# Attention and a mixture of attention experts on one core: later dues for input loads and weights, earlier dues for transposing transfers

## The chip, the cores and the metric

The kernel runs on one core of one Trainium2 chip. The metric is the device time of one execution, in microseconds (us). A core has a matrix engine (TensorE, PE in the profile), a vector engine (VectorE, DVE), a scalar engine for functions such as tanh and exp (ScalarE, ACT), a general engine (GpSimd, POOL) and a small one that issues transfers (SyncE, SP). Each takes its instructions in the order of the program and waits for the others by semaphores. A DMA is a transfer that an engine issues and DMA engines carry out.

## The reference

```python
def _attn_ref(q, k, v, cap):                 # q, k, v: 8 x 12 x 448 x 64, cap = 30
    scores = np.matmul(q, k.transpose(0, 1, 3, 2)) / np.sqrt(64)
    scores = cap * np.tanh(scores / cap)
    attn = softmax(scores)                   # over the last axis
    return np.matmul(attn, v)

x = attn_out.transpose(0, 2, 1, 3).reshape(8, 448, 768)

def _moe_ref(x, w_gate, wq, wk, wv, wo):     # 4 experts, 2 chosen for each row
    logits = x @ w_gate                      # 768 -> 4
    w = softmax(the 2 largest logits)
    for e in range(4):
        q, k, v = x @ wq[e], x @ wk[e], x @ wv[e]        # 768 -> 64
        a = causal_softmax(q @ k.transpose(0, 2, 1) / 8)
        out += chosen(e) * w[e] * (a @ v @ wo[e])        # 64 -> 768
```

The first part is soft-capped attention for 8 batches of 12 heads. Its result x feeds the second part, four small attention experts, of which a gate picks two for each row. The output is 8 x 448 x 768 in 32-bit floats. All inputs are 32-bit; the kernel works in 16-bit floats inside.

## The kernel before

**Pieces.** Two heads make a pair p; there are 48, six to a batch. The pairs of the last batch are cut into two halves of rows, so that there are 54 pieces, numbered from 0; up to 41, piece and pair have one number. A piece goes through these steps:

1. Loads (`load_part`, L273; `add_load`, L314). Two pairs share a set of seven transfers on SP: k, q, two tails of k, v, two tails of v. Pairs 0 to 3 have a list of their own (L306); the others are made by the loop of L328 to L334, for p = 4, 6, 8 and so on, and go into four staging buffers in turn.
2. Casts to 16 bits on POOL (`add_cast`, L362): q (L350), k (L354), v (L360). For pairs 0 and 1 other engines do some.
3. Transposes of q and k (`add_tr`, L431). Up to pair 8 they are matmuls on PE (L398 for q), evicted by DVE. From pair 9 on, k is transposed by a transposing DMA on SP (`a_trd`, L423), and from pair 34 on q is too. "trK" below is the transpose of pair K.
4. Scores (`a_fill`, L502) by PE, into two PSUM tiles in turn, three banks and two banks; so a whole piece takes three tiles, called K.0, K.1 and K.2 in the text.
5. Tanh of each such tile (L513) and one exp for the piece (L522) by ACT.
6. The product with v (PV, L535 and L540) by PE, normalised by DVE (L549, L550), transposed into xT (L563, evicted at L576).

**The mixture.** When all six pieces of a batch are done, `add_batch` (L877) adds its experts: values and gate logits (vps, L620; memset of the value tile's column of ones on POOL, L629, then DVE's copy, L631), the gate on DVE, q and k of the experts (qps and kps, L724), copies of the mask on POOL (mb, L668) that a matmul and DVE turn into masked q, powers for the gate's softmax on POOL (L682 and on), score fills (L743), one exp for each half (L750), causal masking on POOL (L758), PV, o on DVE (L797), additions on POOL (L805), wops (the product with wo, L832), eviction to ob (L846), and a store on SP. The last batch is done half by half (`add_last`, L1160): its late projections are named tX, its last product lwo. The first half of the experts' work of batch b runs beside the attention of batch b + 1.

**Weights.** `add_weight` (L1297) issues them from POOL, as DMAs that turn 32 into 16 bits on the way (L1301): the gate and four wv (into wvg), then two wq and two wk, two wq and two wk, four wo. Their dues are 14, 20, 26 and 32.

**Who sets the order.** The class `Sched` (L25 to L180) is a planner that runs while the program is built. Every step is added as a unit (`add`, L51) with an engine, a duration, the units that it depends on, a `due` (its rank), `after` (a time before which the planner doesn't start it) and, for transfers, `land` (bytes, which the planner sends through a single modelled line of 2.15e5 bytes per us, L107 to L109). The planner keeps a clock for each engine. At each step it takes, among the ready units that could start first on an engine, the one with the smallest due (`pick`, L123). It emits instructions in that planned order. None of these times exists on the chip: only the order does, and the waits for what each instruction uses. Score fills and ACT's work stand outside the dues: fills go in the order of pieces, and other PE work is put between where the plan says that ACT has enough ahead.

Dues come from `nom` (L254 to L259), a nominal start for each piece, about 5.5 us apart in the first batch, and 5.8 after it. A pair's loads are due 40 before its start (L334), and the planner may issue them as soon as their buffer is free. Casts of q and k are due 14 or 20 before, v 4 before; transposes 8 before; transposing DMAs six ahead of that (L447).

```python
        if u["land"]:
            self.dma = max(self.dma, s + 2.0) + u["land"] / 2.15e5
            t = self.dma + 0.1
```

**Semaphores of transfers.** Transfers of SP and ACT use eight semaphores in rotation, and so do the weights on POOL: a transfer waits for the eighth before it.

Of the kernel before, what the change touches and what calls it, by code (L numbers as in the profile page):

```python
# [15 lines left out]
DEBUG = False  # L16
NAUX = 3
PV = (9.0, 5.0, 2.0)
TB = (0.0, 0.0)
PACE = (1.0, 1.0)  # L20
LATE = 3
T0D = -4.0


class Sched:  # L25
# [25 lines left out]
    def add(self, key, eng, dur, deps, due, fn, *args, take=None, give=None, slack=None, land=0,  # L51
            after=0.0, alt=False):
        deps = [d for d in deps if d is not None]
        u = dict(
            key=key, eng=eng, dur=dur, deps=deps, due=due, fn=fn, args=args, take=take, give=give,
            slack=self.SLACK if slack is None else slack, land=land, n=0, r=0.0, after=after, alt=alt,
        )
        self.count += 1
        for d in deps:
            if d not in self.done:  # L60
                u["n"] += 1
                self.wait.setdefault(d, []).append(u)
        if u["n"] == 0:
            self.arm(u)
# [119 lines left out]
def kernel(  # L184
# [13 lines left out]
    nc = tc.nc  # L198

    B, H, S, Dh = q.shape  # L200
# [35 lines left out]
    add = sch.add  # L236
# [24 lines left out]
    def nomp(p):  # L261
        return nom[of[p][0]]
# [38 lines left out]
    def nbytes(n, which):  # L301
        t = {"q": 224 * 0.055, "k": 256 * 0.045, "v": 256 * 0.045}.get(which, 64 * 0.03)
        return n * t / 16 * 2.15e5
# [7 lines left out]
        ("q", 0, 1, "ACT"), ("kt1", 0, 2, "ACT"), ("vt1", 0, 2, "ACT"),  # L311
    ]

    def add_load(p, n, w, due, e, deps):  # L314
        add(
            ("ld", w, p), e, 0.62, deps, due, load_part, p, n, w,
            nc.scalar if e == "ACT" else nc.sync, land=nbytes(n, w),
        )
        for i in range(n):
            ld_of[p + i, w] = ("ld", w, p)  # L320

    last = {}
    for x, (w, p, n, e) in enumerate(FIRST):
        d = [last.get(e)] + ([("zst", w[0], p // 2)] if len(w) > 1 else [])
        d += [("table",)] if e == "ACT" and x > 17 else []
        add_load(p, n, w, -100.0 + x, e, d)
        last[e] = ("ld", w, p, "issued")
    for p in range(4, NP, 2):  # L328
        deps = []
        if p // 2 >= NST:  # L330
            deps = [("cast", w, p - 2 * NST + i) for i in range(2) for w in CASTS]
        for w in PARTS:
            d = deps + [last["SP"]] + ([("zst", w[0], p // 2)] if len(w) > 1 and p < 2 * NST else [])
            add_load(p, 2, w, nomp(p) - 40.0, "SP", d)  # L334

    warm = const.tile([128, 512], f16, name="warm")
    ident = const.tile([128, 128], f16, name="ident")
# [93 lines left out]
    def add_tr(p):  # L431
        deps = [("cast", w, p) for w in "qk"]
        if p >= 8:
            deps += [("filled", i) for i in of[p - 8]]
        due = nomp(p) - (8.0 if p > 3 else 3.5)
        if p == 0:
            for w, d in (("k", "k"), ("q", "q"), ("t", "kt")):
                add(("tr" + w, p), "PE", 0.14 * len(w), [("cast", d, p), ("ident",)], due, a_tr, p,
                    w, take=("tr" + w, p), slack=0.0)
                add(("trev" + w, p), "ACT" if w == "k" else "DVE", 0.4, [("tr" + w, p)], -50.0,  # L440
                    a_trev, p, w, give=("tr" + w, p))
            add(("trev", p), "-", 0.0, [("trevk", p), ("trevq", p)], -50.0, lambda: None)
            add(("tr", p), "-", 0.0, [("trt", p)], -50.0, lambda: None)
            return
        if p >= FIRST_D:
            for w in "qk" if p >= FIRST_Q else "k":
                add(("trd" + w, p), "SP", 1.2, [("cast", w, p)] + deps[2:], due - 6.0, a_trd, p, w,  # L447
                    land=1.05 * 2.15e5)
            if p < FIRST_Q:
                add(("trq", p), "PE", 0.21, [("cast", "q", p)] + deps[2:], due, a_tr, p, "q",  # L450
                    take=("trq", p))
                add(("trdq", p), "DVE", 0.37, [("trq", p)], due + 0.5, a_trev, p, "q",
                    give=("trq", p))
            add(("trev", p), "-", 0.0, [("trdq", p), ("trdk", p)], 0.0, lambda: None)
            add(("tr", p), "-", 0.0, [("trev", p)], 0.0, lambda: None)
            return
        add(("tr", p), "PE", 0.42, deps + [("ident",)], due, a_tr, p, take=("tr", p))
        add(("trev", p), "DVE", 0.58, [("tr", p)], due + 0.5, a_trev, p, "qk", give=("tr", p))
# [418 lines left out]
    def add_batch(b):  # L877
        x = [("xtev", i) for j in range(HP) for i in of[HP * b + j]]
        t0 = nom[HP * (b + 1)] + TB[b == LB - 1]
        pace = PACE[b == LB - 1]  # L880
# [279 lines left out]
    def add_last():  # L1160
# [3 lines left out]
        x0 = [("xtev", i) for i in i0]  # L1164
        t0 = nom[i1[0]] + T0D
        tE = nom[NK]
# [110 lines left out]
    wq2 = [const.tile([128, NDC, 128], f16, name=f"wq2_{r}") for r in range(2)]  # L1277
    wk2 = [const.tile([128, NDC, 128], f16, name=f"wk2_{r}") for r in range(2)]
    wo2 = [const.tile([128, D], f16, name=f"wo2_{r}") for r in range(2)]
    wvg = const.tile([128, NDC, E * Dh + E], f16, name="wvg")  # L1280
# [13 lines left out]
    def rows(w):  # L1294
        return w.rearrange("(c p) m -> p c m", p=128)

    def add_weight(key, pairs, due):  # L1297
        due += 2.0
        for i, (dst, src) in enumerate(pairs):
            def go(dst=dst, src=src):  # L1300
                nc.gpsimd.dma_start(dst, src)  # L1301
            add((*key, i), "POOL", 0.85, [], due + i, go, after=due - 2.0 + i)
        add(
            key, "-", 0.0, [(*key, i) for i in range(len(pairs))], 0.0, lambda: None,
            after=due + 16.0,
        )

    we = range(E)
    cut = [slice(e * Dh, (e + 1) * Dh) for e in we]
    add_weight(  # L1310
        ("w", "wvg"),
        [(wvg[:, :, E * Dh : E * Dh + E], rows(moe_w_gate))]
        + [(wvg[:, :, cut[e]], rows(moe_wv[e])) for e in we], 14.0,
    )
    for r in range(2):
        add_weight(
            ("w", "q", r), [(wq2[r][:, :, cut[g]], rows(moe_wq[2 * r + g])) for g in range(2)], 20.0
        )
        add_weight(
            ("w", "k", r), [(wk2[r][:, :, cut[g]], rows(moe_wk[2 * r + g])) for g in range(2)], 26.0  # L1320
        )
    add_weight(
        ("w", "wo"), [(wo2[e // 2][e % 2 * Dh : (e % 2 + 1) * Dh, :], moe_wo[e]) for e in we], 32.0
    )

    def c_warm():
# [68 lines left out]
    for p in range(NP):  # L1395
        add_cast(p)
        add_tr(p)
# [237 lines left out]
```

## Time and profile before

| what | value |
| --- | --- |
| timed runs | 329.42, 329.1, 326.93 us; median 329.1 |
| profiled execution, whole | 333.61 us |
| its span, first to last instruction | 331.9 us |
| mean granted clock of PE | 0.961 of full |
| instructions | 8178 |
| busy: PE | 281.1 us, 85% of the span |
| busy: ACT | 292.8 us, 88% |
| busy: DVE | 207.2 us, 62% |
| busy: POOL | 173.3 us, 52% |
| data moved by DMA | 52.87 MB, 159 GB/s on average |
| chain that ended last | PE 34%, ACT 26%, DVE 16%, DMA 15%, issue 4% |

The profile is of one execution. Its span runs from its first to its last instruction, and the whole execution is 1.7 us longer. A row of the page's groups gives line, engine, operation, what is written and read, number of instructions, busy time, mean time of one in ns, and the idle time just ahead of these instructions with what ended most of it. A row of a timeline gives start (us from the start of the span), duration, engine, line, operation and operands; in brackets stand the idle time before it and who ended that. The slices are fortieths of the span, 8.3 us each; a digit is the busy share in tenths, and PEclk is PE's granted clock in tenths.

### The profile page before, as it was taken

To read this page: it belongs to the slowest core of one execution; us is meant where nothing else is said; L and a number is where in the kernel's file an instruction comes from. 1 tells how busy PE (TensorE), PEld (TensorE's weight loads), DVE (VectorE), ACT (ScalarE), POOL (GpSimd) and SP (SyncE) were. 2 spreads that over 40 slices of the span, in tenths; PEclk is the share of its full clock that TensorE was granted. 3 is DMA by queue.
4 is the path that set the end of the run, shared out by engine and by line. 5 is a ranking of instruction groups with operands and counts; after the bars stand their busy time and mean duration, and the time that the engine had idled before them with its cause. 6 is when DMAs were issued, how large, how long until landed. Compare 5 with 4: busy or idle time off the path is not lost.

```text
span 331.9 us, 8178 instructions
## 1 busy us (share of the span) xinstructions
PE 281.1 (85%) x3119; PEld 179.6 (54%) x3119; DVE 207.2 (62%) x667; ACT 292.8 (88%) x248; POOL 173.3 (52%) x346
## 2 busy tenths in 40 slices
PE   6886756599889987999899989998799879998873
PEld 2553434257554665557555755566456655676651
DVE  3453322265966758676777687766767576758773
ACT  4889776389999999999999999999999999998252
POOL 5597584649850887247541984298208510741120
PEclk9999569699999999999999999999999999999798
DMA  6999999988999296757697769977352003100035
GB/s 166 261 213 227 244 229 182 232 201 208 207 279 247 58 272 140 202 135 180 177 200 215 148 145 256 225 128 194 63 185 45 0 3 142 28 0 2 20 151 165
DMA packets 93191, 52.87 MB, mean 159 GB/s; under 512 B 53792, under 2 KB 89760, under 8 KB 93152
## 3 DMA queue, kind: packets, MB, share of 16 engines
q1 hardware_dynamic: 81888, 50.19, 64.0%
q0 software_dynamic: 10512, 1.58, 6.7%
q10 hardware_dynamic: 752, 0.59, 0.7%
q8 instruction: 24, 0.39, 0.5%
q14 instruction: 15, 0.12, 0.1%
HBM read 36.19 MB, written 11.01 MB: 142 GB/s over the span
## 4 chain that ended last, share of the span: by engine, by line
PE 34%; ACT 26%; DVE 16%; DMA 15%; issue 4%; SPq 2%; POOL 1%; DVEq 0%; POOLq 0%; ACTq 0%
ACT pbuf L522 12%; ACT y L513 12%; DMA qf<-in_q_dram 8%; PE sc L502 7%; PE pv L540 4%; DMA vst<-in_v_dram 4%; PE sc L743 4%; DVE o L797 3%; PE wops L832 3%; PE qps L724 3%; PE vps L620 3%; DMA kst<-in_k_dram 3%; PE pv L535 2%; PE kps L724 2%; ACT pS L750 2%
## 5 line engine op out<-in xcount | busy, mean ns | idle before, releaser
L513 ACT ACTIVATE y<-sc 128x896 f16<-128x896 f32 (+3 forms) x150 | 144.7, 1057 | 17.6 <-PE sc L502 17.4
L522 ACT ACTIVATE pbuf<-y 128x3136 f16<-128x3136 f16 (+2 forms) x54 | 139.4, 2582 | 0.0
L502 PE MATMUL sc<-qk 64*128 64x448 f16 (+4 forms) x378 | 66.5, 360 | 7.0 <-ACT y L513 4.7
L540 PE MATMUL pv<-v,pbuf 128*128 128x65 f16 x1152 | 61.3, 197 | 0.0
L535 PE MATMUL pv<-v,pbuf 128*128 128x130 f16 x192 | 43.9, 229 | 17.0 <-DVE vs L631 6.3
L540 PEld LDWEIGHTS <-pbuf 128*128 128x128 f16 x1152 | 54.2, 100 | 3.6 <-issue 1.1
L502 PEld LDWEIGHTS <-qk 64*128 64x128 f16 (+1 forms) x378 | 19.9, 95 | 44.4 <-issue 37.5
L668 POOL COPY mb<-mk 128x1024 f16<-128x1024 f16 x14 | 14.1, 1039 | 55.8 <-DVE mk L663 55.8
L350 POOL CAST q<-qf 112x512 f16<-112x512 f32 x46 | 28.1, 614 | 28.7 <-DMA qf<-in_q_dram 28.7
L550 DVE TENSOR_TENSOR xk<-pv,rc 128x256 f16<-128x256 f32 x96 | 40.8, 425 | 3.3
L360 POOL CAST v<-vst 128x512 f16<-128x512 f32 x48 | 29.2, 615 | 10.6 <-PE pv L540 5.5
L535 PEld LDWEIGHTS <-pbuf 128*128 128x128 f16 x192 | 19.2, 100 | 27.6 <-issue 11.5
L846 DVE COPY ob<-wops 128x384 f32<-128x384 f32 (+1 forms) x55 | 28.6, 553 | 4.3 <-PE wops L832 3.8
L576 DVE COPY xT<-xtp 128x448 f16<-128x448 f16 (+2 forms) x51 | 18.3, 366 | 19.8 <-PE xtp L563 19.7
L549 DVE RECIPROCAL rc<-pv 128x4 f32<-128x4 f32 x96 | 17.1, 178 | 21.5 <-PE pv L540 20.9
L620 PE MATMUL vps<-wvg,xT 128*128 128x260 f16 x168 | 28.8, 281 | 0.0
L354 POOL CAST k<-kst 128x512 f16<-128x512 f32 x46 | 28.1, 614 | 0.8 <-DMA kst<-in_k_dram 0.4
L832 PE MATMUL wops<-wo,oT 128*128 128x384 f16 x120 | 26.9, 331 | 0.8 <-DVE ob L846 0.2
L724 PE MATMUL qps<-xT,wq 128*128 128x448 f16 x84 | 23.6, 363 | 0.1
L724 PE MATMUL kps<-xT,wk 128*128 128x448 f16 x84 | 21.9, 352 | 1.2 <-DVE ks L733 0.8
L620 PEld LDWEIGHTS <-xT 128*128 128x128 f16 x168 | 15.9, 100 | 10.9 <-issue 4.2
L682 POOL TENSOR_TENSOR ee<-euler,lg 128x16 f32<-128x16 f32 x7 | 20.4, 2914 | 0.0
(163 smaller groups left out, 427.9 us busy)
## 6 DMA issues: line engine op xcount, KB each, us to landing
qf<-in_q_dram SPq DMA_DIRECT2D x22, 448.0 KB, 5.5
vst<-in_v_dram SPq DMA_DIRECT2D x23, 384.0 KB, 4.9
out_dram<-ob SPq DMA_DIRECT2D x23, 384.0 KB, 2.8
kst<-in_k_dram SPq DMA_DIRECT2D x22, 384.0 KB, 4.3
out_dram<-ob SPq DMA_DIRECT2D x8, 192.0 KB, 2.7
kst<-in_k_dram SPq DMA_DIRECT2D x47, 32.0 KB, 4.8
vst<-in_v_dram SPq DMA_DIRECT2D x47, 32.0 KB, 4.6
kst<-in_k_dram SPq DMA_DIRECT2D x4, 192.0 KB, 3.9
```

The source lines that it names most:

```text
L350: cp(c16["q", p], src.rearrange("p h (c d) -> p c h d", c=QC))
L360: cp(v16[p % NV][:, :, :, 0:Dh], src)
L502: nc.tensor.matmul(o, kk[r, 128 * c : 128 * (c + 1)], qs, start=True, stop=True)
L513: nc.scalar.activation(ytile[i][:, first : first + nb, :], src, AF.Tanh, scale=isc / capf)
L522: nc.scalar.activation(ptile[i], ytile.pop(i), AF.Exp, scale=capf)
L535: nc.tensor.matmul(pv[:, n, :, :], ptile[i][:, idx[0, KC], w : w + 128], v16[p % NV][:, :, KC, :], start=(n == 0), stop=False, skip_group_ ...
L540: nc.tensor.matmul(pv[:, n, g, :], ptile[i][:, idx[g, c], w : w + 128], v16[p % NV][:, g, c, :], start=False, stop=(c == KC - 1), skip_gro ...
L550: nc.vector.tensor_tensor(xk, pv[:, :, :, 0:Dh], rc.broadcast_to((128, 2, 2, Dh)), ALU.mult)
L620: nc.tensor.matmul(ps, xT[b][:, j, w : w + 128], wvg[:, j, :], start=(j == 0), stop=(j == NDC - 1),)
L724: nc.tensor.matmul(s[which, r], w2[r][:, j, :], xT[b][:, j, :], start=(j == 0), stop=(j == NDC - 1),)
L832: nc.tensor.matmul(ps, s["oT"][:, r, w : w + 128], wo2[r][:, f * (D // 2) : (f + 1) * (D // 2)], start=(r == 0), stop=(r == 1),)
L846: cp(s["ob", n][lo:128, f * (D // 2) : (f + 1) * (D // 2)], s.pop(("wops", n, f))[lo:128, :],)
```

## The change

No operation is added or removed. Only what the planner is told differs:

- The loads of pairs 4, 6, 8, 10, 12 and 14 get an earliest time of their own (`EA`), and those of the later pairs one of 36 before their nominal start (`AHEAD`). Before, they had none.
- A transposing DMA is due 12 ahead of its transpose's due instead of 6 (`TD`).
- The weights' dues are 18, 22, 26 and 46 (`WD`) instead of 14, 20, 26 and 32. In the plan each weight now takes its share of the modelled line (1.3 us each), and a group of weights counts as there 10 after its due (raised by 2) instead of 16.
- The mixture of each batch is due 4 later (`TB`), the last one's late part 4 later (`T0D` 0 instead of -4).

```diff
-TB = (0.0, 0.0)
+TB = (4.0, 4.0)
...
-T0D = -4.0
+TD = 12.0
+EA = {4: 0.0, 6: 0.0, 8: 0.0, 10: 24.0, 12: 36.0, 14: 46.0}
+AHEAD = 36.0
+WD = (18.0, 22.0, 26.0, 46.0)
+T0D = 0.0
...
-    def add_load(p, n, w, due, e, deps):
+    def add_load(p, n, w, due, e, deps, after=0.0):
         add(
             ("ld", w, p), e, 0.62, deps, due, load_part, p, n, w,
-            nc.scalar if e == "ACT" else nc.sync, land=nbytes(n, w),
+            nc.scalar if e == "ACT" else nc.sync, land=nbytes(n, w), after=after,
         )
...
-            add_load(p, 2, w, nomp(p) - 40.0, "SP", d)
+            add_load(p, 2, w, nomp(p) - 40.0, "SP", d, EA.get(p, nomp(p) - AHEAD))
...
-                add(("trd" + w, p), "SP", 1.2, [("cast", w, p)] + deps[2:], due - 6.0, a_trd, p, w,
+                add(("trd" + w, p), "SP", 1.2, [("cast", w, p)] + deps[2:], due - TD, a_trd, p, w,
                     land=1.05 * 2.15e5)
...
-            add((*key, i), "POOL", 0.85, [], due + i, go, after=due - 2.0 + i)
+            add((*key, i), "POOL", 0.85, [], due + i, go, after=due - 2.0 + i, land=1.3 * 2.15e5)
         add(
             key, "-", 0.0, [(*key, i) for i in range(len(pairs))], 0.0, lambda: None,
-            after=due + 16.0,
+            after=due + 10.0,
         )
...
-        + [(wvg[:, :, cut[e]], rows(moe_wv[e])) for e in we], 14.0,
+        + [(wvg[:, :, cut[e]], rows(moe_wv[e])) for e in we], WD[0],
...
-            ("w", "q", r), [(wq2[r][:, :, cut[g]], rows(moe_wq[2 * r + g])) for g in range(2)], 20.0
+            ("w", "q", r), [(wq2[r][:, :, cut[g]], rows(moe_wq[2 * r + g])) for g in range(2)], WD[1]
...
-            ("w", "k", r), [(wk2[r][:, :, cut[g]], rows(moe_wk[2 * r + g])) for g in range(2)], 26.0
+            ("w", "k", r), [(wk2[r][:, :, cut[g]], rows(moe_wk[2 * r + g])) for g in range(2)], WD[2]
...
-        ("w", "wo"), [(wo2[e // 2][e % 2 * Dh : (e % 2 + 1) * Dh, :], moe_wo[e]) for e in we], 32.0
+        ("w", "wo"), [(wo2[e // 2][e % 2 * Dh : (e % 2 + 1) * Dh, :], moe_wo[e]) for e in we], WD[3]
```

## The prediction

> **What bounds the kernel now.** I read the page first, slice by slice:
>
> ```profile
> ACT  4889776389999999999999999999999999998252
> POOL 5597584649850887247541984298208510741120
> PEclk9999569699999999999999999999999999999798
> ```
>
> From slice 9 (75 us) to slice 35 ScalarE is full: its tanh and exp set the pace there. It is not full between 33 and 66 us and in the last 28 us. The waits of ACT, in 0 to 125 and in 125 to 265 us, put a number on it:
>
> ```profile
> ACT y L513 <- PE sc L502: 16.9, 12, 6.6
> ```
> ```profile
> ACT y L513 <- PE sc L502: 0.5, 1, 0.5
> ```
>
> Nearly all stall is early, and every time on score matmuls. The timelines of ACT, PE and POOL in 27 to 66 us tell why they were late:
>
> ```profile
> 39.74 2.91 ACT L513 ACTIVATE y<-sc 128x1344 f16<-128x1344 f32 x3 [1.72 <-PE sc L502]
> 47.13 2.15 ACT L513 ACTIVATE y<-sc 128x896 f16<-128x896 f32 x2 [1.77 <-PE sc L502]
> 50.95 0.92 ACT L513 ACTIVATE y<-sc 128x896 f16<-128x896 f32 x1 [1.67 <-PE sc L502]
> 63.18 0.92 ACT L513 ACTIVATE y<-sc 128x896 f16<-128x896 f32 x1 [6.62 <-PE sc L502]
> ```
> ```profile
> 36.77 0.55 PE L398 MATMUL tr<-ident,q 112*128 112x112 f16 x4 [2.15 <-POOL q L350]
> 45.44 0.56 PE L398 MATMUL tr<-ident,q 112*128 112x112 f16 x4 [3.99 <-POOL q L350]
> 61.99 0.27 PE L535 MATMUL pv<-v,pbuf 128*128 128x130 f16 x1 [6.32 <-DVE vs L631]
> ```
> ```profile
> 31.50 0.82 POOL L1301 DMA_DIRECT2D wk<-in_moe_wk_dram  x1 [0.85 <-DMA wvg<-in_moe_wv_dram]
> 34.73 0.82 POOL L1301 DMA_DIRECT2D wk<-in_moe_wk_dram  x1 [2.41 <-DMA wvg<-in_moe_wv_dram]
> 36.10 0.62 POOL L350 CAST q<-qf 112x512 f16<-112x512 f32 x1
> 44.26 0.51 POOL L1301 DMA_DIRECT2D wo<-in_moe_wo_dram  x1 [1.31 <-DMA wq<-in_moe_wq_dram]
> 44.76 0.62 POOL L350 CAST q<-qf 112x512 f16<-112x512 f32 x1
> 59.60 0.61 POOL L350 CAST q<-qf 112x512 f16<-112x512 f32 x1 [6.02 <-DMA qf<-in_q_dram]
> 61.27 0.12 POOL L629 MEMSET vs<- 128x6 f16 x1
> ```
>
> The casts at 36.10 (q of piece 7) and 44.76 (piece 8) had their loads long since; they stood in POOL's queue behind weight DMAs that waited for older weight DMAs. PE had their transposes ahead of scores that were ready, so ScalarE starved. At 53 us POOL waits for the load of pair 14, eight pieces before its use; behind it stands the memset of batch 0's value tile, behind that DVE's copy, behind that PE's vps banks, and the scores of piece 8. That is the 6.62. Order in queues bounds this stage; bytes do not.
>
> **What the Trainium skill says.** "DMA: Bandwidth & Descriptors", "Anatomy of one DMA": a semaphore wait is taken on the issuing sequencer, the DMA engines don't wait. So POOL stands still in 31 to 45 us; the trace agrees (0.85 and 2.41 us above). Same page, "Queues, rings and completion order": each DMA engine takes turns between queues packet by packet. The trace agrees: 96 KB of weights take 10.6 to 19.1 us to land beside loads of 384 to 448 KB that take 4.3 to 5.5. "TensorE: Matmul & The Clock Gate", Part 1: the clock is low after idleness; here it is 0.66 in 30 to 50 us.
>
> **The change part by part.** In the built program no instruction is added or removed; only order changes. "Held back" is in the planner alone: on the chip a load starts when SP reaches it. SP's first 44 DMAs (through pair 10) keep their order.
>
> *POOL's weights.* They now come behind six casts. q4's load lets it start at 19.66 as before; with k4, q5, k5 at 0.556 apart POOL is at 21.9. Gate DMA 1.06, four wv and two wq at 0.83: 27.9. v4, third wq: 29.3. The fourth waits for the gate weights (7.6 us to landing: 29.5): 30.3. q6, k6: 31.4. Now the four wk wait for the four wv. The first is issued at 23.0 and lands 10.5 later (median of wvg), 33.5; before, POOL's waits ended at 31.5, 34.7, 39.4 (two transfers on), 41.8, 44.3, so one lands each 2.4 or so; a first gap of 1 to 2 makes the fourth 39.5. Bounds: 36.6 (issue 25.4 plus the longest, 11.2) and 43.1 (3.2 each). I take 39.5. Behind it are v5, q7, k7, v6, q9, k9, q8, k8: q7 is cast at 41.4, q8 at 44.1 instead of 36.10 and 44.76. POOL is not faster here.
>
> *PE's order.* tr6 stands behind piece 4's scores, tr7 behind those of piece 5, so tanh 5.1 and 5.2 run at 38.0 without the 1.72. Then scores 6.0 stand behind tr7 (41.5 to 42.7, 1.2 us as before), tr of q9 (43.7), four PV groups of piece 4 (1.5 at the low clock): 45.2, plus 0.5. Tanh 6.0 runs at 45.8, exp 5 at 46.6 to 49.3 (before 42.5 to 45.2): 4.1 us worse at this point. It is then repaid: tr8 and scores 6.1, 6.2 hide under exp 5, so there is no 1.77; scores 7.0 under tanh 6.1, 6.2, so no 1.67. Exp 6 runs at 52.0 against 51.76: even.
>
> *Memset and held loads.* Pair 12's load moves behind the transposing DMA of k9, pair 14's behind those of k10, k11; their casts now stand behind batch 0's masks. So POOL from 44.7 does seven casts (3.9), one wo (0.5), and the memset at 49.2 instead of 61.27. DVE wants it at about 54: five us of cover. Scores 8.0 come at 55.9, tanh 7.1, 7.2 end at 56.6, and tanh 8.0 runs at 56.6 instead of 63.18: **-6.6**. Weights: the last wq lands near 39.5+4x2.4 = 49.1, wanted at 53; the last wk near 58.7, wanted at 60. The second cover is thin.
>
> *Transposes.* k9's DMA leaves SP at 43.7 instead of 45.87 and lands before 50 (it took 3.2 median, 8.9 at 45.87); scores 9.0 want it at 61. With TD 12 and loads at -36, load (8 us first issue to last landing), cast and transpose leave ten us or more before the scores. Behind a transpose waiting on SP stand loads and stores; loads have that margin, stores none to keep. No cost.
>
> *Batch 0's masks.* PE now has tr of q12 and q13 ahead of a mask score fill. From the mask (62.3 by the same count): two copies 2.0, the power 2.94, q12, k12, seven small ops 2.56, then q13: done 71.6; PE is there at 69.4. It waits 2.2, then needs 1.4; ScalarE is out of work at 72.7, so about **+1.1**. The old stalls of this stretch, 1.39+0.16+0.58, go: **-2.1**.
>
> *90 to 300 us.* ScalarE has 0.6 us idle and PE 7 to 8% to spare; the same work in an order that still puts attention first (TB 4 puts the mixture later): 0. Unseen; bounds -0.5 and +6 (1 us in each of six batches).
>
> *The end.* Exp 53 ended at 303.4; the last projections tX began 11.5 later, held by the xT of piece 50, whose PV came at 310.8. In the new order this PV stands right behind piece 53's, ahead of the lpv groups. On DVE from 0.5 after exp 53: two o triples 1.9, five gate ops 1.0, xk 53 0.6, four gate ops 0.8, xk 50 0.6, oscL 0.8: tX at about 7, 4.5 earlier. Given back: twelve wops evictions behind tX where seven were, 0.5 each on two engines, and three more on DVE beside the last lwo: 1.3+1.5. I take **-2.0**; bounds -3.5 and +1.5 (tX not earlier, evictions paid).
>
> Sum: -6.6+1.1-2.1-2.0 = -9.6. The profiled execution spans 331.9 (333.6 with what lies around it): 322.3 and 324.0. The timed runs have a median of 329.1, 4.5 below it; the same difference gives **319.5**.
>
> **Rivals.** *Weights become the wait.* They start 5.7 us later at the same rate. If one lands each 2.8 to 3.2 us, the wv wait costs up to 3.6 more at tanh 6.0, and the last wk comes at 62 to 65 where kps wants it at 60. For: waits of 2.41 and 19.1 to landing. Against: SP has nothing to load from about 38 until the transpose at 43.7, so the weights are alone for a while. Gain 3 to 5: 324 to 326.
> *POOL blocks PE in every batch (slower).* Casts used to be far ahead; now q casts stand directly before or behind masks, the power and o additions, and PE's transposes of q wait for them in order. The place is the stretch of mask scores in batches 0 to 5; the price is 1.1 in batch 0; PE can lose about 2.7 us of a 35 us batch for nothing. If each of the six lost 1.6 the gain is gone, and above 2.2 it is slower by 1%: at 2.5, 329.1-9.6+15 = 334. Against: POOL is half idle, mb alone waited 55.8 us for its mask, and waits of 8.3 for a load in mid-run cost ScalarE nothing before.
> *It does not do what it says.* Loads aren't held by time, DMA is shared: 329. Against: POOL's order at the memset does differ.
> *Better.* wv lands at 36.6, the end gives 3.5: 6.6+2.8+1.0+3.5, 315.
>
> **How the numbers follow.** The sum as forecast 0.58 (its own range 316 to 323), better 0.14, weights 0.18, no change 0.05, POOL blocking 0.05. Eight in ten: 313.5 to 325.5. About 1% (3.3 us) is what a measurement here tells from no change. Faster takes the first two and nearly all of the third; within 1% no change and the rest; slower POOL blocking: 0.87, 0.08, 0.05.
>
> **What would show it.** Right: no ACT wait of over 2 us in 50 to 70, the memset near 49, ACT's waits before 125 us down from 16.9 to 10 or less with the longest near 46, exp 53 some 7.6 earlier, tX within 8 of it. Wrong: kps waiting for wk near 60, PE waiting for POOL q in several batches, ACT waits over 3 us in all in 125 to 265, a last part of 28 us or more.

## The result, and the profile after

The change makes the kernel a little faster, by less than half of what was forecast. In the first comparison the kernel after took 325.01 us (median of 4 runs, 324.86 to 325.38) and the kernel before 328.96 (4 runs, 326.93 to 329.42): a ratio of 0.989 (0.985 to 0.994), 4.0 us less. In a later comparison on one chip after ran at 326.60 (4 runs, 322.74 to 327.32), before at 331.07 (7 runs): 0.984 (0.977 to 0.991), 4.5 us less. The profiled executions stand further apart: spans of 331.9 and 323.7, 8.2 us. The ratios here and below leave out runs over 1.5% longer than the fastest of their kernel; medians and ranges keep them.

The page of after, in slices of 8.1 us:

```profile
ACT  4889989999999999999999999999989999996251
POOL 6479880797409941595538750695549410833020
PEclk9579579999999999999999999999999999999798
```

From slice 6 to slice 35 ScalarE is all but full; the hole of before, between 33 and 66 us, is closed. The waits of ACT in 0 to 125 and in 125 to 265 us:

```profile
ACT y L517 <- PE sc L506: 4.9, 7, 1.5
```
```profile
ACT y L517 <- PE sc L506: 2.7, 4, 1.1
```

16.9 became 4.9, but 0.5 became 2.7. The timeline of after between 33 and 66 us shows what became of the stalls that were forecast to go, and of the one that was forecast to come:

```profile
34.77 0.82 POOL L1305 DMA_DIRECT2D wk<-in_moe_wk_dram  x1 [1.31 <-DMA wvg<-in_moe_wv_dram]
...
41.37 0.92 ACT L517 ACTIVATE y<-sc 128x896 f16<-128x896 f32 x1 [1.48 <-PE sc L506]
44.47 0.14 POOL L633 MEMSET vs<- 128x6 f16 x1
...
64.47 0.92 ACT L517 ACTIVATE y<-sc 128x896 f16<-128x896 f32 x1 [0.60 <-PE sc L506]
```

The memset comes at 44.47 instead of 61.27, the 6.62 before tanh 8.0 is gone, and the new stall at tanh 6.0 is there, at 1.48. Where the 8.2 us between the two profiles come from is read off the starts of the exps, which both kernels run in one order:

| start of exp | before | after | difference |
| --- | --- | --- | --- |
| 5 | 42.52 | 42.18 | -0.34 |
| 6 | 51.76 | 47.77 | -3.99 |
| 7 | 63.99 | 53.46 | -10.53 |
| 11 | 90.33 | 78.38 | -11.95 |
| 24 | 165.79 | 153.72 | -12.07 |
| 39 | 252.48 | 243.50 | -8.98 |
| 53 | 302.12 | 292.96 | -9.16 |
| end of the span | 331.9 | 323.7 | -8.2 |

So 11.95 us are won by 90 us, 2.8 given back in the middle and 0.9 at the end (29.4 behind exp 53 instead of 28.5).

### The profile page after: what moved, and what is told of

Same layout as the page of the kernel before. It is cut to its first block, busy times and chain, and to the rows that moved or that the text cites. A ratio compares the mean times of both kernels' runs of the same rounds, so it can differ in the third digit from the quotient of the medians.

```text
span 323.7 us, 8173 instructions
## 1 busy us (share of the span) xinstructions
PE 278.2 (86%) x3119; PEld 178.3 (55%) x3119; DVE 206.3 (64%) x667; ACT 292.6 (90%) x248; POOL 173.2 (54%) x346
## 4 chain that ended last, share of the span: by engine, by line
PE 24%; DMA 19%; DVE 15%; ACT 15%; POOL 14%; SPq 7%; issue 4%; DVEq 0%; POOLq 0%; ACTq 0%
ACT pbuf L526 7%; ACT y L517 6%; DMA qf<-in_q_dram 6%; DMA out_dram<-ob 6%; PE sc L506 4%; PE pv L544 3%; DMA vst<-in_v_dram 3%; DMA wvg<-in_moe_wv_dram 3%; SPq L294 3%; PE wops L836 3%; POOL q L354 3%; SPq L303 3%; DVE ob L850 2%; PE vps L624 2%; DVE o L801 2%
## 5 line engine op out<-in xcount | busy, mean ns | idle before, releaser
L506 PE MATMUL sc<-qk 64*128 64x448 f16 (+4 forms) x378 | 64.6, 349 | 4.8 <-ACT y L517 2.8
L850 DVE COPY ob<-wops 128x384 f32<-128x384 f32 (+1 forms) x56 | 29.6, 554 | 10.0 <-PE wops L836 5.0
L364 POOL CAST v<-vst 128x512 f16<-128x512 f32 x48 | 28.6, 620 | 9.1 <-DMA vst<-in_v_dram 8.8
L624 PE MATMUL vps<-wvg,xT 128*128 128x260 f16 x168 | 27.9, 274 | 0.0
L728 PE MATMUL kps<-xT,wk 128*128 128x448 f16 x84 | 20.9, 352 | 2.8 <-DVE ob L850 1.5
L728 PE MATMUL qps<-xT,wq 128*128 128x448 f16 x84 | 22.6, 352 | 0.3 <-DVE qs L737 0.3
L567 PE MATMUL xtp<-perm,xk 128*128 128x128 f16 x144 | 18.2, 227 | 4.2 <-DVE xk L554 2.6
```

The costliest lines, as they stand in the source:

```text
L364: cp(v16[p % NV][:, :, :, 0:Dh], src)
L506: nc.tensor.matmul(o, kk[r, 128 * c : 128 * (c + 1)], qs, start=True, stop=True)
L624: nc.tensor.matmul(ps, xT[b][:, j, w : w + 128], wvg[:, j, :], start=(j == 0), stop=(j == NDC - 1),)
L728: nc.tensor.matmul(s[which, r], w2[r][:, j, :], xT[b][:, j, :], start=(j == 0), stop=(j == NDC - 1),)
L850: cp(s["ob", n][lo:128, f * (D // 2) : (f + 1) * (D // 2)], s.pop(("wops", n, f))[lo:128, :],)
```

## The experiments

Theory 1 is that of the prediction: the early stage hangs on POOL's queue, in which casts and a memset stand behind weight transfers and a cast whose load is late; the change reorders that queue. The rivals: the profiled execution of before was unlucky; one part carries the whole; the end or the mixture's dues decide. One part needs no run: with TD at 6 instead of 12 the kernel after becomes the same program on all five queues, instruction for instruction. So the earlier dues of the transposing transfers do nothing beside the other parts; what they would do without them was not run.

| kernel | median us (runs) | range | ratio to before, interval |
| --- | --- | --- | --- |
| before again | 331.51 (20) | 327.6 to 335.5 | 1.002 (0.998 to 1.006) |
| before, memset on DVE | 329.33 (21) | 325.9 to 333.7 | 0.996 (0.993 to 0.999) |
| before + TB | 330.58 (10) | 328.0 to 332.6 | 1.006 (1.000 to 1.012) |
| before + holds | 330.71 (10) | 329.1 to 333.6 | 1.001 (0.997 to 1.004) |
| before + weights | 332.87 (2) | 329.9, 335.8 | none |
| after without new weights | 336.45 (4) | 335.7 to 338.1 | 1.021 (1.011 to 1.030) |
| after without holds | 333.04 (20) | 328.7 to 337.3, one apart | 1.006 (1.003 to 1.010) |
| after with TB 0, T0D -4 | 330.06 (12) | 327.3 to 335.8 | 0.999 (0.995 to 1.003) |
| the same, slack 2.5 | 328.02 (20) | 325.3 to 332.3 | 0.994 (0.990 to 0.997) |
| after again | 326.60 (4) | 322.7 to 327.3 | 0.984 (0.977 to 0.991) |
| after, T0D -4 | 321.55 (4), 325.51 (4) | 321.3 to 327.9 | 0.979 (0.970 to 0.987), 0.986 (0.979 to 0.992) |
| after, T0D -8 | 322.68 (4), 324.98 (4) | 322.4 to 326.7 | 0.976 (0.971 to 0.981), 0.980 (0.973 to 0.987) |
| after, T0D -8, wk 30 | 322.43 (4), 322.56 (4) | 320.4 to 325.5 | 0.974 (0.969 to 0.979), 0.968 (0.960 to 0.975) |
| the same, slack 1.2 | 329.12 (5) | 328.6 to 329.2 | 0.991 (0.987 to 0.994) |

### How much the kernel before varies

No edit but four blank lines.

> The kernel before, unchanged but for four blank lines (so that line numbers match those of the kernel after). Theory 1, the profiled execution of before is typical and its 6.62 us stall at 63 us is always there: the profile shows exp 8 at about 71.0 and ScalarE waits of some 16.9 us in 0 to 125, and the timed runs are faster than the profile for another reason (the end, or the middle). Theory 2, that execution was an unlucky one, in which loads or weights landed late: the profile shows exp 8 at 66 to 68.5, waits in 0 to 125 of 12 to 14.5, and an execution of 327 to 330 us; the rest of the run within 0.5 us of the profile of before from exp 9 to exp 53.

The profiled execution was like the first (333.45; exp 8 at 69.45, the stall before tanh 8.0 at 6.55), so theory 1 holds for the trace. But the timed runs spread over 8 us, and their middle lies higher than the first ones shown: 331.5 here, 330.8 in 47 runs of the unchanged file beside them, against the 329.1 that the prediction subtracted from. None of the profiles caught before itself at 327 to 329, so what a short execution saves, and where, isn't shown. The nearest is before + TB (330.64 in its profile), whose stall at this place was 4.29. The profiled executions of three kernels with this early stage were long ones for their kernel: 333.45 here, 333.74 with the memset on DVE and 333.55 with the holds alone, against medians of 331.5, 329.3 and 330.7. Those of after were not (325.38 and 326.18 against 325.01 and 326.60). Whether a profiled execution of the early stage of before waits longer for its loads than the timed ones stays open.

After again, as it is:

> The kernel after, unchanged. Theory 1 (the change takes away what varies: its early stage no longer hangs on when single loads and weights land): the runs stay within 2 us of 325.0. Rival (the first four runs, 324.9 to 325.4, were lucky; the kernel that shares its first 60 us, loads and weights alone with slack, ran 325.3 to 332.3 and showed a stall of 4.5 at 44 us when a weight landed 3 us later): a spread of 4 us or more, 325 to 330, and a profile that may show PE waiting over 2 us for POOL's q at 36 to 42 us.

The rival was nearer: a spread of 4.6 us, and a longer stall at tanh 6.0, where the prediction had placed one. The timeline of after again, 34 to 45 us:

```profile
37.07 0.82 POOL L1305 DMA_DIRECT2D wk<-in_moe_wk_dram  x1 [1.55 <-DMA wvg<-in_moe_wv_dram]
...
39.11 0.56 PE L402 MATMUL tr<-ident,q 112*128 112x112 f16 x4 [2.04 <-POOL q L354]
...
43.66 0.92 ACT L517 ACTIVATE y<-sc 128x896 f16<-128x896 f32 x1 [2.61 <-PE sc L506]
```

The fourth wk waits for the fourth wv, which landed some 2.3 us later than in the first profile of after; behind it stands the cast of q of piece 7, behind that its transpose on PE, behind that the scores of tanh 6.0. That delay stays: exp 11 is 2.35 later.

### The memset alone, on the kernel before

```diff
-            nc.gpsimd.memset(s["vs"][:, :, 0 : VW : VW - 1], 1.0)
+            nc.vector.memset(s["vs"][:, :, 0 : VW : VW - 1], 1.0)
```

> The kernel before with the memset of the mixture's value tile issued by DVE just ahead of DVE's own copy, instead of by POOL (same work, 7 instructions moved from one engine to the other). Theory 1 (the stall before tanh 8.0 is the memset standing behind POOL's wait for the load of pair 14): the stall goes from 6.6 to under 1.5, exp 8 comes 4 to 6 earlier, and 1 to 2 of it are lost in batch 0's masks, whose copies still stand behind the same wait of POOL: 324 to 326. Rival (the load itself, or weights for qps and kps, are the next wait at the same place): exp 8 within 1.5 of the unchanged kernel, 328 to 330.

The stall before tanh 8.0 went, and exp 8 came 6.5 us earlier (64.48). Theory 1 was right on that, and wrong on what was left: at exp 9 only 0.8 of it remained, and the time, 329.3, is what the rival had named. The timeline, 60 to 77 us:

```profile
61.92 0.62 POOL L354 CAST q<-qf 112x512 f16<-112x512 f32 x1 [7.22 <-DMA qf<-in_q_dram]
...
70.48 0.50 PE L709 MATMUL mps<-ident,mb 128*128 128x128 f16 x3 [4.39 <-POOL mb L672]
...
75.14 0.92 ACT L517 ACTIVATE y<-sc 128x896 f16<-128x896 f32 x1 [5.81 <-PE sc L506]
```

POOL's wait for the load of pair 14 is still there, 7.22 us (6.02 in the profile of before). The next thing that stands behind it, the mask copies mb, now holds PE and then ScalarE for 5.81. Taking one victim out of the queue hands the wait to the next; the wait itself must be moved.

### Each part alone, and each left out

Before with TB 4 only:

> The kernel before with only the mixture's dues 4 later (TB 4; loads, transposes, weights and T0D as before). Theory 1 (TB helps only where PE would wait for POOL's o additions, and before has only 1.6 us of such waits in 75 to 285; the stall at 63 us stays): exp 8 stays near 70, waits of ScalarE before 125 us stay at 13 to 17, and the time is 329 to 333. Rival (TB carries the gain of the change by itself): waits before 125 us under 9, 324 to 327.

As theory 1 said: 330.6, exp 8 at 69.74, waits before 125 us of 15.3.

Before with the loads' earliest times only:

> The kernel before with only the loads' earliest times (weights, transposing transfers, TB and T0D as before). Theory 1 (holds without later weights leave POOL standing behind weights at 31 to 45, and take away its early loads as cushion): exp 8 at 64 to 67, waits of 3 or more in the middle, 330 to 336. Rival (holds carry the gain by themselves): exp 8 at 59 to 62, 324 to 327.

As theory 1 said on the whole: 330.7. The late stall is gone (exp 8 at 63.78) and the weights' waits are there as before (exp 6 at 51.87); later 2.79 and 1.48 are lost elsewhere.

Before with the weights only:

> The kernel before with only the weights changed (later dues, their share of the modelled line, there after 10). Theory 1 (weights alone free POOL early, but the mixture of batch 0 then stands ahead of the scores of piece 9, as in after without holds): memset before 54, exp 7 at 53 to 57, exp 9 at 71 to 75, 328 to 334. Rival (weights carry the gain by themselves): exp 9 at 65 to 68, 324 to 327.

Two runs, 329.9 and 335.8; the profile is of the longer. Memset at 47.96, but 4.37 lost at tanh 6.0 and 5.10 at 66.81: not faster.

After with the weights as before:

```diff
-WD = (18.0, 22.0, 26.0, 46.0)
+WD = (14.0, 20.0, 26.0, 32.0)
...
-            add((*key, i), "POOL", 0.85, [], due + i, go, after=due - 2.0 + i, land=1.3 * 2.15e5)
+            add((*key, i), "POOL", 0.85, [], due + i, go, after=due - 2.0 + i)
...
-            after=due + 10.0,
+            after=due + 16.0,
```

> The kernel after with the weights as in the kernel before (dues 14, 20, 26, 32, no share of the modelled line, there 16 after the due); holds, TB, TD and T0D as after. Theory 1 (weights ahead of casts make POOL stand still in 31 to 45 us, and hold up the casts of pieces 7 and 8): POOL waits of 3 or more for older weights, exp 6 at 50 or later instead of 47.8, and 2 to 4 us of it stay to the end: 327 to 329. Rival (what blocks is the loads' order alone): exp 8 within 1 of 59.1, 324.5 to 326.

It is worse than theory 1 said, and slower than before: 336.5. Its timeline, 33 to 48 us, has the picture of before back:

```profile
34.41 0.82 POOL L1305 DMA_DIRECT2D wk<-in_moe_wk_dram  x1 [2.34 <-DMA wvg<-in_moe_wv_dram]
...
44.09 0.51 POOL L1305 DMA_DIRECT2D wo<-in_moe_wo_dram  x1 [1.30 <-DMA wq<-in_moe_wq_dram]
45.27 0.37 PE L402 MATMUL tr<-ident,q 112*128 112x112 f16 x4 [3.27 <-POOL q L354]
46.86 2.14 ACT L517 ACTIVATE y<-sc 128x896 f16<-128x896 f32 x2 [1.14 <-PE sc L506]
```

Exp 6 is 3.5 later than in after, exp 7 6.2, exp 11 8.0 and exp 39 11.0, in an order that differs as a whole.

After without the loads' earliest times:

```diff
-            add_load(p, 2, w, nomp(p) - 40.0, "SP", d, EA.get(p, nomp(p) - AHEAD))
+            add_load(p, 2, w, nomp(p) - 40.0, "SP", d)
```

> The kernel after without the earliest times of the loads (they may be planned as soon as their buffer is free, due 40 before their piece, as in the kernel before); weights, TB, TD and T0D as after. Theory 1 (the held loads put batch 0's memset ahead of the casts of pair 14, and keep the transposing transfers from standing behind loads): the memset on POOL at 55 or later, a ScalarE wait of 3 to 6 before tanh 8.0, exp 8 at 63 to 66, 328 to 331. Rival (with the weights later POOL reaches the memset in time anyway): the memset before 54, exp 8 within 1 of 59.1, 324.5 to 326.

Its profile caught an execution of 602.6 us, far from all others (328.7 to 337.3), and is not read. A second profile:

> The kernel after without the earliest times of the loads, again, for a trace (333.0 median in the timed runs before). Theory 1 (the memset stands behind the cast of pair 14 and its load): memset on POOL at 55 or later, a ScalarE wait of 3 to 6 before tanh 8.0. Rival (the memset is in time, and the 8 us over after come from waits spread over the early stage or from the middle): memset before 54, no wait of over 3 before tanh 8.0, exp 8 near 60 and waits of 5 or more after 70.

Neither theory was right as it stood. There is a wait of 4.68, but it is one piece later than theory 1 said, before tanh 9.0, and the memset is early. The time, 333.0, is above the 328 to 331 named for it. The timeline, 44 to 65 us:

```profile
45.42 0.13 POOL L633 MEMSET vs<- 128x6 f16 x1
...
63.42 0.55 PE L506 MATMUL sc<-qk 64*128 64x448 f16 x4
63.89 0.92 ACT L517 ACTIVATE y<-sc 128x896 f16<-128x896 f32 x1 [4.68 <-PE sc L506]
```

PE is busy with hardly a pause from 54.95 to 63.4: it runs the mixture of batch 0 (vps, qps, kps, PV, mps) and only then the scores of piece 9, though the k of this piece had landed at 50.8. In after, two score fills stand in that stretch, at 57.80 and 59.58. The holds thus act on PE too, through the plan's order. That the planner puts the scores back because unheld loads fill its modelled line ahead of this transposing transfer is how the code reads; no run took the line alone away.

After with TB 0 and T0D -4, that is, loads and weights alone:

> The kernel after with all mixture dues as before (TB 0, T0D -4): the change is then loads and weights alone. Theory 1 (loads and weights carry the whole gain; TB costs the 2.8 us that were given back between exp 9 and exp 53): exp 53 is 1.5 to 3 earlier than in after, its end part 28 to 29, 322.5 to 324. Rival (TB carries part of the gain at 60 to 125 us, where stalls of 2.1 went): ScalarE waits 2 or more in 60 to 125 again, and 325 to 327.

The rival, and more: 330.1, the whole gain gone, though exp 10 is where it is in after (72.73 against 72.91). What is lost comes later: a wait of 2.00 at 79.55, and 4.2 between exp 29 and 39. PE waits 6.1 us in 4 places for POOL's addition of o ahead of its transpose; in after 2.4 in 3. The same with 2.5 of slack for that transpose:

```diff
-            add(("oT", b), "PE", 0.46, [("oa", b)], tb(26.0), s_ot, b, take=("oT", b))
+            add(("oT", b), "PE", 0.46, [("oa", b)], tb(26.0), s_ot, b, take=("oT", b), slack=2.5)
```

> The kernel of the run with loads and weights alone (TB 0, T0D -4), where PE waited 6.1 us in 4 places for POOL's addition of o ahead of its transpose and the granted clock then fell to 0.5 to 0.68; here the planner is told that this transpose may start 2.5 later after the addition, and nothing else. Theory 1 (those waits, and the low clock behind them, are what the mixture's later dues save): PE's waits for POOL's o under 2 us, no slice under 9 in PEclk after 75 us, exp 53 near 291 to 293 instead of 298.8, 321 to 324, with a spread under 3 us. Rival (the clock falls for another reason, or the waits move to another place): 326 or more, with low slices of PEclk after 75 us again.

In between, and no proof: the wait left the list and ScalarE's waits after 125 us fell from 7.1 to 1.9, but those in 75 to 125 rose from 2.0 to 4.8, with PE waiting 2.2 once for DVE's o. This execution also lost 4.50 at tanh 6.0, its fourth wk issued at 37.67.

So no part is shown to be worth anything alone (the weights alone have two runs), and with any of the three out the gain is gone. Each of these kernels also has an order of its own behind the part that differs, so that what one part is worth isn't shown; that all three are needed is. As the traces show it, they take away waits that stand behind one another: weights ahead of casts (31 to 45 us), the load of pair 14 ahead of memset and masks (53 to 61), mixture ahead of scores.

### The end

```diff
-T0D = 0.0
+T0D = -4.0
```

> The kernel after with the last batch's late part due 4 earlier again (T0D -4 as before; all else as after). Theory 1 (the end got longer by the 4 later, since more evictions of the last-but-one batch now stand behind the late projections): from the end of exp 53 to the last instruction 27 to 28.5 instead of 29.4, 323 to 324.5. Rival (the end is set by the order of TB, or by a chain that does not depend on these dues): within 0.7 of after, 324.5 to 325.5.

> The kernel after with T0D -4, again, beside after on the same chip. Theory 1 (the last batch's late part 4 later lengthens the end by 2 to 3.5): 2 to 3.5 under after in the same call, its part behind exp 53 near 27 instead of 29.4. Rival (the gap of 3.5 in the earlier call was between lucky and unlucky early stages): within 1 of after, and the part behind exp 53 differs by under 1.

And with -8:

> The kernel after with T0D -8 instead of 0: the last batch's late part 8 earlier. Theory 1 (the end is set by how much of the last-but-one batch's evictions and of late transposes stands ahead of the last projections; the earlier the better): the part behind exp 53 is 25 to 27, and the time 0 to 1.5 under that with -4. Rival (with -8 this work stands ahead of the last scores and delays exp 53 by what it saves): within 0.7 of the one with -4, or slower by 1 to 2, with ScalarE waits before exp 53.

> The kernel after with T0D -8, again, as the partner of the one with wk due 30 on the same chip. Theory 1 (the end is 2 us shorter than that of after in every execution, the early stage varies by up to 4): a median of 322 to 325 with a spread of 2 to 5. Rival (the 322.6 to 324.2 of the earlier call is the whole of its spread): within 321.5 to 324.5.

The part behind exp 53 is 27.2 twice with -4, 27.3 and 27.4 with -8 (28.4 and 27.4 in the two profiles below, whose order is the same there), against 29.4 and 28.6 with 0: about 1.5 to 2 us, and no more from -8. One such figure is good to about 1 us: the 28.4 holds 3.4 us at half the clock that the other three with -8 don't. So the part that theory 1 named for -4 came (27 to 28.5), and the one for -8 (25 to 27) did not. In time -4 was first 3.5 below after, but those runs were not taken together; beside each other on one chip the gap was 1.1, which is within the spread of four runs. Where the end loses time shows in windows (length, then busy us and count of PE, PEld, DVE, ACT, POOL; granted clock, DMA share, GB/s). After:

```profile
299.00:303.00 4.00, 2.17 (x23) 1.90 (x24) 3.21 (x13) 0.76 (x3) 0.48 (x1) 0.79 0.00 0
303.00:308.00 5.00, 4.15 (x37) 3.15 (x37) 2.59 (x9) 1.77 (x7) 0.00 (x0) 0.83 0.01 3
```

and with T0D -8:

```profile
299.00:303.00 4.00, 3.65 (x43) 2.57 (x43) 3.22 (x8) 1.54 (x4) 1.15 (x1) 1.00 0.17 59
303.00:308.00 5.00, 4.23 (x42) 2.81 (x39) 3.07 (x11) 2.73 (x8) 0.42 (x2) 1.00 0.30 115
```

In after PE is half idle in 299 to 303, mostly waiting for DVE's normalisation (1.43 us at 300.71), the granted clock is at half from 301.30 to 304.71, and the sixteen tX that begin at 302.63 take 2.5 us instead of the 1.5 of before. Stores also begin there with -8, and not in after.

### What is left

T0D -8 and the four wk due 30:

```diff
-WD = (18.0, 22.0, 26.0, 46.0)
+WD = (18.0, 22.0, 30.0, 46.0)
```

> The kernel after with T0D -8 and the four wk due 30 instead of 26, which moves two things only: the casts of v of piece 5 and of q and k of piece 7 stand ahead of the four wk on POOL instead of behind them. Theory 1 (what is left of the early variation is the time at which POOL, waiting with a wk for older weights, reaches the cast of q of piece 7, as in the profile of after again, where PE waited 2.04 for it): no PE wait of over 1 for POOL's q at 36 to 42 us, no ScalarE wait of over 1 at 41 to 45, 0.8 to 2.5 under the one with T0D -8 alone in the same call, and a smaller spread. Rival (the wk land that much later and kps waits for them at 56 to 58; or the early variation comes from loads): within 0.7 of it or slower, with a wait of kps for wk.

> The kernel with T0D -8 and wk due 30, again, as partner on the same chip. Theory 1 (its early stage no longer hangs on the weights): a median of 321.5 to 323.5, and no ScalarE wait of over 1 at 40 to 45 us in its profile. Rival (the first four runs were lucky): a median over 324.

As theory 1 said, but for the spread. On POOL only the casts named move; on PE and DVE the transpose of piece 7 moves with them. Its medians are among the lowest: 322.4 beside 325.0 for its partner, and 322.6 on another chip. That it is faster than -8 alone isn't shown: the ranges on the one chip overlap (321.3 to 325.1 and 322.4 to 326.7), and -8 alone ran at 322.7 elsewhere. The wait at tanh 6.0 is gone in both profiles. The timeline of the first, 33 to 46 us, and ACT's waits in 0 to 125:

```profile
34.47 0.82 POOL L1305 DMA_DIRECT2D wk<-in_moe_wk_dram  x1 [0.92 <-DMA wvg<-in_moe_wv_dram]
...
39.62 0.37 PE L402 MATMUL tr<-ident,q 112*128 112x112 f16 x4
```
```profile
ACT y L517 <- PE sc L506: 3.8, 7, 1.0
```

A wk still waits 0.92 for older weights; nothing that PE needs soon stands behind it. The spread stays (320.4 to 325.5): the two profiles differ by 0.1 at exp 24, by 2.1 at exp 31 behind a wait of 2.09 at 195 us, at the transpose of o, and by 1.6 at exp 53. With slack 1.2 for that transpose:

> The kernel with T0D -8 and wk due 30, and the planner told that the transpose of o may start 1.2 later after POOL's addition (it stands that much later in PE's order). Theory 1 (what is left in the middle is PE standing at this transpose, 1.8 us in 3 places, and the low clock after the longer of these waits): PE's waits for POOL's o under 0.7, ScalarE waits of under 1 in 125 to 265 instead of 1.9, 0.5 to 1.5 under its partner. Rival (a planner's order moves as a whole; the waits turn up in another place, as in the run with 2.5): within 0.7 of the partner or slower.

The rival came true, strongly: 329.1 beside 322.6. The wait went and others came (PE 4.3 us for the eviction of wops, ScalarE 7.1 in 125 to 265 instead of 3.1). An edit that moves one unit in the plan reorders all after it, so neither slack run shows what the wait alone is worth.

## Why the prediction was wrong

The sign was right, and on the profiled executions the sum was near: -9.6 forecast, -8.2 found. It was reached by errors of both signs, so that its nearness is luck, and the step from the profile to the timed runs failed.

- *"The same difference gives 319.5."* This step failed. It took the 4.5 us between the profiled execution of before and the median of its three runs for something that the change leaves alone. The change does not: the profiled execution of after, 325.4, stands 0.4 above its median, so that 8.2 us between the two profiled executions are 4 between the medians. The execution that was read was a long one. In later comparisons, on five chips, the middle of before is 330.7 to 332.5, so that its 333.6 lies 1 to 3 above the middle, and its stalls were counted in full. The rest of the 4.5 is that the first runs of before lay lower, at 329.1. That can be the luck of three runs, or of the place where they ran, since after too was 1.6 lower there than in the later comparison; the runs don't tell these apart. Of the 5.6 us that the forecast was off (9.6 against 4.0), this step holds some 4.2 and the terms below 1.4.
- *Weights* (fourth wv at 39.5, bounds 36.6 to 43.1). It landed at 34.5 in the first profile, below the bound, and at 36.8 in after again. The gaps were about right: 5.7 us from the first wv to the fourth, where 6.0 were forecast. The first landing was mis-sized. The 10.5 us of before were carried over though the transfers around it had moved; it took 6.0 (issued at 22.73, landed at 28.76), and 8.5 in after again. The place was right: tanh 6.0 is where after waits longest before 125 us, 1.48 (2.61 in after again) instead of the 5.9 that the forecast implied, from 39.9 to 45.8. Exp 6 came at 47.8, not 52.0.
- *Memset and held loads* (-6.6). Right: at 44.47 instead of the forecast 49.2, and the stall is gone. That moving the load's wait was needed, and not the memset alone, is shown by the run with the memset on DVE.
- *Batch 0's masks* (+1.1 and -2.1). 0.60 and 0.21 of waits were found: near. To exp 11 the sum forecast -7.6 and the profile has -11.95; nearly all of the 4.3 is the weights' step (4.2 by exp 6).
- *Transposes, no cost.* Right, and trivially so: TD changes nothing in the program of after.
- *90 to 300 us* (0, bounds -0.5 and +6). +2.8. Its rival was right in kind for a part, POOL ahead of PE; but PE waits mostly for the addition of o (2.4 us in 3 places), less for casts of q (1.2 in 2).
- *The end* (-2.0, bounds -3.5 and +1.5). +0.9. Projections tX began 8.35 after exp 53 instead of 11.5 (forecast 7), and 12 evictions stand behind them, as forecast. From the start of tX to the end it takes 21.0 us instead of 17.0: 4.0 given back where 2.8 were counted; 1.0 of it is the low clock under tX, which no term held.
- *The rival "Weights become the wait"* named 324 to 326, and 325.0 came; that is luck. The weights landed earlier than forecast, not later, and near 60 kps waited for no wk (its one wait there is 0.21, for DVE).

Of the marks set beforehand, two for the early stage held (no ACT wait over 2 in 50 to 70, 4.9 before 125); the memset at 44.5 instead of 49, the longest wait at 41 instead of 46 and tX 8.35 behind exp 53 instead of 8 missed. A last part of 28 or more was a mark of being wrong, and it came.

How the middle loses its 2.8 is clear only in part. ScalarE's waits in 125 to 265 us are 2.2 longer than before. The timeline of after, 190 to 196 us, shows one of the four:

```profile
191.87 0.34 PE L819 MATMUL otS<-ident,o 128*128 128x128 f16 x3 [1.26 <-POOL o L809]
...
193.21 1.15 PE L836 MATMUL wops<-wo,oT 128*128 128x384 f16 x6 [0.50 <-DVE oT L829]
...
195.17 0.92 ACT L517 ACTIVATE y<-sc 128x896 f16<-128x896 f32 x1 [0.79 <-PE sc L506]
```

PE stands 1.26 us at the transpose of o, and then has wops and a PV group ahead of the scores. A wait of 0.48 at 159.08 follows such a transpose too. The longest of the four, 1.09 at 242.69, does not: PE had stood 0.62 us for an eviction of xT at 241.38, with kps of the next mixture ahead of the scores. The waits behind a transpose of o thus come to 1.3 of the 2.8. That the order with TB 4 loses less in the middle than that with TB 0 is measured; what the wait at the transpose alone costs is not, since both runs that took it away moved other waits.

## What to carry to other kernels

Where an engine issues transfers and also does work that others need, ask of every wait in its queue what stands behind it; taking one victim out hands the wait to the next, so move the waiting instruction, and all of them, before you expect a gain. A profile is one execution: before you subtract its stalls from a median, see how far the runs of that kernel spread and whether the stalls are what varies. An order that a planner makes moves as a whole, so a change of one due is tested by the trace, not by its intention.

## What the runs showed of the hardware

The granted clock falls without a long pause. In the profile of T0D -8 again, 190 to 198 us:

```profile
192.98 0.34 PE L819 MATMUL otS<-ident,o 128*128 128x128 f16 x3 [1.80 <-POOL o L809]
...
194.32 2.10 PE L836 MATMUL wops<-wo,oT 128*128 128x384 f16 x6 [0.50 <-DVE oT L829]
...
197.45 0.92 ACT L517 ACTIVATE y<-sc 128x896 f16<-128x896 f32 x1 [2.49 <-PE sc L506]
```

After a pause of 1.80 and one of 0.50 the six wops take 2.10 us, where after 1.26 and 0.50 they took 1.15 (after, above), and ScalarE waits 2.49 instead of 0.79: with a pause half a microsecond longer, 1.7 more are lost. Another profile agrees: a ScalarE wait of 2.09 after a pause of 2.03 with wk 30 again.

The traces show what decides. In all of them the granted clock is either full or half, and changes only on a grid of 3.41 us. In T0D -8 again PE was busy for 1.55 us of the step from 190.48 to 193.89, and the next step was at half; in after the step with the pause of 1.26, from 188.66 to 192.07, has 2.11, and the clock stayed full. The same stands ahead of tX in after: 1.41 us of work from 297.89 to 301.30, then half. Between 60 and 300 us the 19 profiles (without that of 602.6) have 20 falls from full to half. Each came after a step with 1.95 us of work or less; all 14 steps with 1.79 or less were followed by a fall, and none with 1.96 or more; in between both happen. Before 60 us there are falls after up to 2.37. What a pause costs thus hangs on where it lies on the grid and on how much PE works around it. The ends of matmuls are modelled in a profile, so these figures are approximate.

The Trainium skill, "TensorE: Matmul & The Clock Gate", Part 1, says that the clock falls after an idle window of some 3.4 us that runs freely. The length agrees with the 3.41 here. But the window need not be idle: 1.8 us of work in it did not keep the clock up.
